# Four column tiles for the small products of a recurrent attention, and wide-attention steps moved to the front

## The chip, the cores and the metric

The kernel runs on one core of a Trainium2 chip. A core has a matrix engine (TensorE, "PE" in the profile; its weight loads are "PEld"), VectorE ("DVE"), ScalarE ("ACT"), GpSimd ("POOL"), a queue engine (SyncE, "SP") and 16 DMA engines. The metric is device time in microseconds; lower is better.

TensorE's array has 128 rows and 128 columns. It can be used whole ("full" below, 128*128 in the profile) or in tiles that work side by side: 128*64 is half the columns ("half"), 128*32 a quarter of them ("col"), 64*128 half the rows ("tall"), 32*128 a quarter of the rows ("row"). Four products that fill the four quarters are called a quartet here.

## The reference

Two attentions over the same 2048 tokens are mixed by a gate per token. The first is recurrent: 64 segments of 32 tokens, each with 8 memory tokens in front, and the first 8 output rows of a segment are the memory of the next. The second is a plain softmax attention with 32 heads of 18.

```python
def _A_ref(x, mem0, Wq, Wk, Wv, Wo, seg_len):      # 32 heads of 128, Dm 576
    ...
    for s in range(n_seg):                          # 64 segments
        xs = x[:, s * seg_len:(s + 1) * seg_len, :].copy()
        h = jnp.concatenate([mem, xs], axis=1)      # 8 + 32 tokens
        q = jnp.einsum('btd,dhe->bhte', h, Wq)
        k = jnp.einsum('btd,dhe->bhte', h, Wk)
        v = jnp.einsum('btd,dhe->bhte', h, Wv)
        scores = jnp.einsum('bhqe,bhke->bhqk', q, k) * scale
        scores = jnp.where(mask[None, None], scores, -1000000000.0)
        p = _softmax(scores, axis=-1)
        o = jnp.einsum('bhqk,bhke->bhqe', p, v)
        o = jnp.einsum('bhte,hed->btd', o, Wo)
        mem = o[:, :M, :].copy()
        outs.append(o[:, M:, :])
    return jnp.concatenate(outs, axis=1)

g = _sigmoid((x * gate_w).sum(-1, keepdims=True))
a = _A_ref(x, A_mem0, A_Wq, A_Wk, A_Wv, A_Wo, A_seg_len)
b = _B_ref(x, B_wqkv, B_wo)                         # softmax attention, 32 heads of 18
return g * a + (1 - g) * b
```

## The kernel before, in words

**The order is planned.** Nothing is issued as it is written. Every operation is handed to `add` with its engine, an assumed duration, what it depends on, a priority and, for TensorE, the tile mode. `Plan.run` then places the operations one by one on five engines by these assumed durations, and the instructions are emitted in that order, so each engine's queue is fixed when the program is built. Among the operations that can start, the lowest priority number goes first; for TensorE a change of tile mode adds `RANK["switch"]`. Most priorities come from the table `RANK`. Where the plan sees TensorE wait for long enough while a wide-attention accumulation is open, it puts in a filler: a product of zeros that adds nothing to the bank `ob` (`warm_col`, L773, and `warm_full`, L779; "obW" and "filler" below).

**First stage.** All tokens are transposed (ptx). TensorE computes the wide attention's queries and keys (pq, `project_qk`, 36 units of five products) and values (pvb, `project_v`, 32 units). The evacuations of these units, in the order in which they are written, are the list `beats`. The results go through DRAM (qtd, ktd, vgd) and come back as tiles of one group of four heads (qch, kch, vch). `load_weights` brings the recurrent weights in 12 slices (Wv, then Wq, then Wk, four each) on GpSimd's DMA queue; slice number k waits for evacuation 2 + 4k, by a marker that VectorE writes (L530). The gate's products are pgs. When the first stage's memory is free, `open_rest` opens the second stage's tiles with memsets on GpSimd.

**The wide attention** is 512 visits: 8 groups of four heads, 4 chunks of 512 queries (group and chunk together are `gq`, 0 to 31), 16 blocks of 128 keys. A visit is four row-tiled products of scores into sb (L801), one exponential over 128x2048 on ScalarE into etb (L810), and four column-tiled products with the values into ob (L819). There is one sb buffer of four banks, so the next scores wait for the exponential. After 16 visits VectorE normalises the chunk and GpSimd stores it (otd).

**The recurrence** is 64 steps. In each, 8 memory tokens and the first 24 new tokens (32 in all) are projected: Q, K and V in two halves, each of five quartets with 512 columns (pvv, L1126). Q and K are transposed by DMA (tt<-tm, issued on SP) and copied into qk. The last 8 tokens of a segment need no memory, so their projections are done apart: the *last units* (`last_unit`, pv, L896 and L900), one for each of 4 groups of 16 segments (q), of Q, K and V, and of 8 column blocks. A value unit is five products with 512 columns, a Q or K unit 20 products with 128. They go through DRAM (vld, qkd) and return as xl and v_sb. Then, for each half of the heads: scores psh (L1215, 16 products of 64 columns of weights by 40), exponential, masking by a minimum, sums over each pair of heads pss (L1241, three full products by 2), reciprocal, spreading prb (L1258, six half products by 128), multiplication, values pso (L1279, tall), copies to ot, and the output projection acc (L1040, quartets by 144). The fold (pw, L1327 to L1329, three full products) turns the first 8 output rows back into the next step's input ht. Every fourth step the last tokens' outputs are projected too.

**Pacing.** `seg_gate[s]` is the first pvv of step s. The first `RANK["ahead"]` visits are free of it (62 before); the others are spread evenly over the 64 steps, each tied to its step's gate. Last units of group q + 1 are handed in during the 16 steps of group q, 24 over 15 of the 16.

**The end.** The recurrent output is read back from DRAM, GpSimd multiplies its 16 blocks of 128 tokens by the gate (L1469), TensorE does the wide output projection (po, L1482 and L1486), VectorE adds both, and SP stores.

Of the kernel before, what the change touches and what calls it, by code (L numbers as in the profile page):

```python
# [16 lines left out]
RANK = {  # L17
    "switch": 0.563, "near": 0, "early": 0.35, "wait": 0.363, "Q0": 1.228, "K0": 2.187, "Q1": 3.003,
    "K1": 2.432, "V0": 4.793, "V1": 5.753, "t0": 4.121, "t1": 0.488, "ph0": 6.882, "ph1": 0.05, "sm0": 1.292,
    "sm1": 0.349, "bc0": 1.798, "bc1": 1.166, "po0": 0.486, "po1": 0.474, "op0": 6.496, "op1": 0.107,  # L20
    "fo": 0.097, "lo0": 9.11, "lo1": 2.155, "la": 2.226, "ob": 0.587, "eQ": 8.858, "eK": 1.861, "eV": 1.477,
    "co": 0.886, "le": 6.512, "xp": 7.097, "mn": 0.05, "ct": 3.886, "fin": 16.522, "la_gate": 1, "lo_gate": 1,
    "ahead": 62, "behind": 0, "tail": 0.404, "qc": 2.731, "gap": 0, "cool": 7.325,
}


class Op:
# [3 lines left out]
        "engs", "dur", "fn", "deps", "prio", "mode", "take", "give", "tail",  # L31
        "eng", "start", "end", "left", "users", "name", "seq", "slots", "dmas", "kb",
    )
# [11 lines left out]
class Plan:  # L45
# [42 lines left out]
    def add(  # L88
        self, name, engs, dur, fn, deps=(), prio=5.0, mode=None, take=(), give=(), tail=0.0, dmas=0, kb=0.0
    ):  # L90
        op = Op(name, engs, dur, fn, deps, prio, mode, take, give, tail)
        op.dmas, op.kb = dmas, kb
        op.seq = len(self.ops)
        op.slots = {}
        self.ops.append(op)
        return op
# [7 lines left out]
    def run(self):  # L104
        free = self.free = {e: 0.0 for e in ("PE", "DVE", "ACT", "POOL", "SP")}
        waiting = {e: [] for e in free}
        mode = None
# [8 lines left out]
        order = []  # L116
        n = len(self.ops)
# [5 lines left out]
        while len(order) < n + extra:  # L123
# [11 lines left out]
            if pick == "PE" and open_ and self.warm is not None:  # L135
                for m in ("col", "full"):
                    if m not in (mode, op.mode):
                        continue
                    turn = 0.0 if mode == m else self.SWITCH
                    done = sum(d for t, d in recent if t > free["PE"] - 2.5)  # L140
                    if est - free["PE"] < self.WARM + turn + RANK["gap"] or done > RANK["cool"]:
                        continue
                    w = Op("warm", "PE", self.WARM, self.warm[m], [], 9.0, m, (), (), 0.0)
                    w.dmas, w.kb, w.slots, w.left = 0, 0.0, {}, 0
                    w.eng, w.start, w.end = "PE", free["PE"], free["PE"] + self.WARM + turn
                    free["PE"], mode = w.end, m
                    recent.append((w.end, self.WARM))
                    order.append(w)
                    extra += 1
                    pick = None  # L150
                    break
                if pick is None:
                    dirty = {"PE"}
                    continue
# [7 lines left out]
            if pick == "PE":  # L162
                if op.mode != mode:
                    dur += self.SWITCH
                mode = op.mode
                if op in self.opens:
                    open_ = True
                if op in self.closes:
                    open_ = False
                recent = recent[-8:]  # L170
                recent.append((est, dur * self.ARRAY[mode]))
            op.end = est + dur
# [86 lines left out]
def kernel(  # L259
# [15 lines left out]
    nc = tc.nc  # L275
# [252 lines left out]
    def behind(name, beat, corner, n, fn, deps, tail):  # L528

        mark = add(f"mk{name}", "DVE", 0.07, lambda e: nc.vector.memset(corner(), 0.0), [beat, *deps], prio=0.05)  # L530
        before = paced[-1:]
        op = add(name, "POOL", 0.7 * n, fn, [mark, *deps, *before], prio=0.15, tail=5.5)
        paced.append(op)
        return op

    def load_weights():
        k = 0
        for w, src, name in ((wv, A_Wv, "wv"), (wq, A_Wq, "wq"), (wk, A_Wk, "wk")):
            w2 = src.rearrange("d h e -> d (h e)")
            weight_loads[name] = []  # L540
            for c in range(NF):
                def load_w(e, w=w, w2=w2, c=c):
# [10 lines left out]
                weight_loads[name].append(  # L553
                    behind(f"{name}{c}", beats[2 + 4 * k], lambda w=w, c=c: w[0][0:1, 0, c, 0:1], 3, load_w, [], 5.5)
                )
# [230 lines left out]
    for gq in range(GB * NQC):  # L786
        g, qc = divmod(gq, NQC)
        load_q(gq)
        for kb in range(NKB):
# [15 lines left out]

            vi = add(f"sb{gq}.{kb}", "PE", 0.216, visit, [k_of[c], q_of[gq], last_vi], prio=0.0, mode="row", take=("sb",))

# [6 lines left out]
            def values(e, c=c, gq=gq, kb=kb, o=o):  # L814
# [11 lines left out]
            va = add(  # L826
                f"ob{gq}.{kb}", "PE", 0.216, values, [ex, v_of[c], last_va], prio=RANK["ob"], mode="col",
                take=("ob",) if kb == 0 else (), give=(("etb", ex, 0),),
# [54 lines left out]
    last_ops = []  # L883

    def last_unit(q, kind, b, prio, gate_dep):
        cols = slice(q * P, (q + 1) * P)
        j, hf = divmod(b, 2)

        def part(k):
            def fn(e):  # L890
# [3 lines left out]
                if kind == 2:  # L894
                    rw, cc = w_slice(wv, k, b * 512, 512)
                    nc.tensor.matmul(pv[:, :], lhsT=xL[:, cc, cols], rhs=rw, start=(k == 0), stop=(k == NF))  # L896
                    return
                for c in range(NF + 1):
                    lw, cc = w_slice((wq, wk)[kind], c, (4 * b + k) * Dh, Dh)
                    nc.tensor.matmul(  # L900
                        pv[:, k * P:(k + 1) * P], lhsT=lw, rhs=xL[:, cc, cols], start=(c == 0), stop=(c == NF)
                    )
            return fn
# [5 lines left out]
        for k in range(NF + 1 if kind == 2 else NF):  # L909
            a = add(  # L910
                f"la{tag}.{k}", "PE", 0.216 if kind == 2 else 5 * 0.057, part(k), [a] if a else deps,
                prio=prio - (0.01 if a else 0.0), mode="full", take=() if a else ("pb",),
            )
            parts.append(a)
# [56 lines left out]

    opening = add("open", "POOL", 5.0, open_rest, b_work + early, prio=0.5)

# [81 lines left out]
    group_end = {}  # L1055
    pend_lo = []

    for s in range(n_seg):
# [124 lines left out]
        for hf in range(2):  # L1183
# [25 lines left out]
            def psh(e, hf=hf, s=s):  # L1209
                box["psh", s, hf] = ph = bank([P, W8], FP32, "psh")  # L1210
                qk = opened["qk"]
                for r in range(8):
                    for jj in range(2):
                        k = jj * 8 + r
                        nc.tensor.matmul(  # L1215
                            ph[64 * jj:64 * jj + 64, r * L:(r + 1) * L],
                            lhsT=qk[:, hf, 1, k * L:k * L + 64], rhs=qk[:, hf, 0, k * L:(k + 1) * L],
                            start=True, stop=True, tile_position=(0, 64 * jj),
                        )

            p_ = add(f"ph{hf}.{s}", "PE", 0.41, psh, [*turned, pl], prio=RANK[f"ph{hf}"], mode="half", take=("pb",))
            cur[f"psh{hf}"] = p_

# [14 lines left out]
            def sm(e, hf=hf, s=s):  # L1238
                box["pss", s, hf] = ps = bank([P, 6], FP32, "pss")
                for k, o in enumerate(CH):  # L1240
                    nc.tensor.matmul(  # L1241
                        ps[:, 2 * k:2 * k + 2], lhsT=opened["et", hf][:, o:o + P], rhs=bsel[:, :], start=True, stop=True
                    )

            s_ = add(f"sm{hf}.{s}", "PE", 0.1, sm, [m_], prio=RANK[f"sm{hf}"], mode="full", take=("pb",))

# [7 lines left out]
            def bc(e, hf=hf, s=s):  # L1254
                box["prb", s, hf] = pr = bank([P, W8], FP32, "prb")
                for k, o in enumerate(CH):
                    for jj in range(2):
                        nc.tensor.matmul(  # L1258
                            pr[64 * jj:64 * jj + 64, o:o + P],
                            lhsT=box["rq", s, hf][:, 2 * k + jj:2 * k + jj + 1].to_broadcast([P, 64]),  # L1260
                            rhs=ident[:, :], start=True, stop=True, tile_position=(0, 64 * jj),
                        )

            b_ = add(f"bc{hf}.{s}", "PE", 0.2, bc, [r_], prio=RANK[f"bc{hf}"], mode="half", take=("pb",))

# [57 lines left out]
        if s + 1 < n_seg:  # L1323
            def fold(e, s=s):
                box["pw", s] = pw_ = bank([P, NF + 2, M], FP32, "pw")
                obf, bd = box["obf", s], opened["bd"][:, :, :].rearrange("p a r -> p (a r)")
                nc.tensor.matmul(pw_[:, 0:NF, :], lhsT=obf[:, 0:P], rhs=selm, start=True, stop=True)  # L1327
                nc.tensor.matmul(pw_[:, NF, :], lhsT=bd[:, TL:3 * TL], rhs=sel[:, :], start=True, stop=True)
                nc.tensor.matmul(pw_[:, NF + 1, :], lhsT=bd[:, 0:2 * TL], rhs=sel[:, :], start=True, stop=True)  # L1329

            fo = add(f"fo{s}", "PE", 0.1, fold, [c1, c2], prio=RANK["fo"], mode="full", take=("pb",))
            cur["fold"] = fo
# [51 lines left out]
        if i4 == 3:  # L1384
            lo_deps = [hist[s - k]["otl"] for k in range(4)]
            pend_lo.append((s, gi, lo_deps))
            if s == n_seg - 1:
                last_out(*pend_lo.pop(), None)
        if s < 48:
            q = s // 16 + 1  # L1390
            lo, hi = (s % 16) * 24 // 15, min(24, (s % 16 + 1) * 24 // 15)
            if s % 16 == 15:
                lo = hi = 24
            order = [(2, b) for b in range(8)] + [(k, b) for b in range(8) for k in (0, 1)]
            for kind, b in order[lo:hi]:
                last_unit(q, kind, b, RANK["la"], gates_of[RANK["la_gate"]])


# [160 lines left out]
```

## Time and profile before

| what | us |
|---|---|
| median of three runs (1497.04 to 1503.77) | 1502.29 |
| the profiled execution's own time | 1500.88 |
| its span | 1499.2 |
| first visit's scores start | 45.0 |
| first step's first projection (pvv) starts | 136.05 |
| last product (pw) of the fold of step 0, 46, 62 | 180.4, 1130.8, 1443.4 |
| ScalarE, 512 exponentials over 128x2048, 1.877 each | 961.2 busy |
| TensorE, fillers L773 and L779 | 60.6 and 24.6 busy |
| last weight slice issued | 129.3 |

The profile is one execution. Its page gives the busy time of each engine, then the span in 40 slices of 37.5 us with a digit for the busy tenths, the granted clock of TensorE ("PEclk", tenths of full speed) and the share of DMA. A timeline lists instructions in order of time: start, length, engine, line, operation, output<-inputs, tile of the array as rows*columns, shape, count, and in brackets the idle time before it with what ended it. Matmuls of one queue overlap, so lengths do not add up; distances between starts do.

### The profile page before, as it was taken

What the parts mean: (1) busy time and instruction counts of PE and PEld (TensorE: products, weight loads), DVE (VectorE), ACT (ScalarE), POOL (GpSimd) and SP (SyncE); (2) the same over time, 40 slices, a digit from 0 to 9 for tenths busy, and PEclk for the clock granted to TensorE, in tenths of its full rate; (3) what the DMA queues carried; (4) which work ended last, traced back from release to release, by engine and by line L of the source; (5) the groups of instructions that cost most, each with busy time, mean ns of one, the idle gap of its engine ahead of it and who ended that gap; (6) DMA issues with size and microseconds to landing.
All of it is one profiled execution on the core that took longest, in us unless ns stands there. A gap on an engine that the chain in (4) does not pass through costs nothing.

```text
span 1499.2 us, 68540 instructions
## 1 busy us (share of the span) xinstructions
PE 1388.5 (93%) x30405; PEld 763.4 (51%) x30435; DVE 833.4 (56%) x2033; ACT 1053.4 (70%) x760; POOL 553.2 (37%) x1166
## 2 busy tenths in 40 slices
PE   7689899999999999999999999999999999998997
PEld 4345444555555445555555544555554545454445
DVE  6244455665655555665555555565655555554555
ACT  2125687777777787777777877777777777776770
POOL 7222124423352324433352325333453225333235
PEclk9799999999999999999999999999999999999999
DMA  8865633433233333333333333323333324333344
GB/s 269 260 233 171 163 64 77 74 58 67 59 75 68 59 61 70 75 66 61 69 69 60 70 54 79 69 57 68 71 73 80 53 57 68 59 56 47 47 112 125
DMA packets 343380, 130.09 MB, mean 87 GB/s; under 512 B 296943, under 2 KB 329159, under 8 KB 343083
## 3 DMA queue, kind: packets, MB, share of 16 engines
q1 hardware_dynamic: 314843, 81.22, 28.1%
q0 software_dynamic: 27088, 43.31, 10.7%
q8 instruction: 238, 3.90, 1.1%
q10 hardware_dynamic: 1152, 1.18, 0.3%
q14 instruction: 59, 0.48, 0.1%
HBM read 52.74 MB, written 30.86 MB: 56 GB/s over the span
## 4 chain that ended last, share of the span: by engine, by line
PE 66%; ACT 13%; DMA 10%; DVE 6%; issue 3%; POOL 1%; SPq 0%; ACTq 0%; DVEq 0%
PE pvv L1126 24%; ACT etb L810 13%; PE sb L801 11%; PE acc L1040 8%; PE ob L819 7%; DMA tt<-tm 6%; PE pv L900 4%; PE pq L608 2%; PE psh L1215 2%; DVE tm L418 2%; PE pv L896 2%; PE ob L773 1%; PE pso L1279 1%; DMA vgd<-vt 1%; PE prb L1258 1%
## 5 line engine op out<-in xcount | busy, mean ns | idle before, releaser
L810 ACT ACTIVATE etb<-sb 128x2048 bf16<-128x2048 f32 x512 | 961.2, 1877 | 332.6 <-PE sb L801 311.7
L418 DVE CAST tm<-pvv 128x512 bf16<-128x512 f32 x360 | 248.3, 691 | 256.8 <-PE pvv L1126 250.0
L1126 PEld LDWEIGHTS <-ht 128*32 128x32 bf16 x7680 | 206.8, 97 | 185.2 <-DVE ht L1335 10.6
L801 PE MATMUL sb<-qch,kch 32*128 32x512 bf16 x2048 | 205.8, 386 | 33.7 <-ACT etb L810 20.3
L819 PE MATMUL ob<-etb,vch 128*32 128x512 bf16 x2048 | 205.3, 390 | 1.9 <-issue 1.4
L1077 POOL COPY ht<-xg 128x96 bf16<-128x96 bf16 x64 | 17.3, 270 | 418.2 <-PE pvv L1126 398.9
L1040 PE MATMUL acc<-wo,ot 128*32 128x144 bf16 x8192 | 160.4, 228 | 3.2 <-issue 2.3
L1040 PEld LDWEIGHTS <-ot 128*32 128x32 bf16 x8192 | 135.3, 97 | 23.0 <-issue 9.2
L801 PEld LDWEIGHTS <-kch 32*128 32x128 bf16 x2048 | 65.5, 91 | 149.0 <-issue 121.8
L1126 PE MATMUL pvv<-wq_m,ht 128*32 128x512 bf16 x2048 | 140.2, 380 | 0.8 <-DVE ht L1335 0.8
L1126 PE MATMUL pvv<-wv_m,ht 128*32 128x512 bf16 x2048 | 139.6, 379 | 0.7 <-DVE tm L418 0.7
L1126 PE MATMUL pvv<-wk_m,ht 128*32 128x512 bf16 x2048 | 136.5, 379 | 0.9 <-DVE vl L418 0.9
L418 DVE CAST ot<-pso 128x320 bf16<-128x320 f32 x216 | 98.6, 482 | 54.7 <-PE pso L1279 54.3
L819 PEld LDWEIGHTS <-vch 128*32 128x32 bf16 x2048 | 53.0, 93 | 103.2 <-issue 101.7
L1199 DVE COPY qk<-tt 128x512 bf16<-128x512 bf16 x256 | 76.7, 306 | 43.1 <-DMA tt<-tm 40.7
L1095 POOL COPY qk<-xl 128x256 bf16<-128x256 bf16 x128 | 50.4, 401 | 92.8 <-PE psh L1215 79.4
L1268 DVE TENSOR_TENSOR et<-et,prb 128x320 bf16<-128x320 bf16 x128 | 61.2, 480 | 36.0 <-PE prb L1258 33.5
L722 POOL DMA_DIRECT2D qch<-qtd x120 | 60.8, 514 | 49.1 <-PE sb L801 45.4
L722 POOL DMA_DIRECT2D otd<-stage x124 | 62.6, 512 | 31.6 <-DVE stage L862 26.4
L1166 DVE COPY v_sb<-tm 32x512 bf16<-32x512 bf16 x234 | 70.5, 301 | 6.1 <-ACT tm L416 0.3
L722 POOL DMA_DIRECT2D kch<-ktd x112 | 56.7, 513 | 43.4 <-PE sb L801 43.2
L1215 PEld LDWEIGHTS <-qk 128*64 128x64 bf16 x2048 | 45.0, 112 | 51.4 <-issue 38.8
(149 smaller groups left out, 1860.7 us busy)
## 6 DMA issues: line engine op xcount, KB each, us to landing
xl<-qkd SPq DMA_DIRECT2D x64, 128.0 KB
v_sb<-tm SPq DMA_DIRECT2D x256, 32.0 KB
qkd<-vl POOLq DMA_DIRECT2D x48, 128.0 KB, 2.7
wo<-in_A_Wo_dram POOLq DMA_DIRECT2D x4, 1152.0 KB, 8.8
vgd<-vt SPq DMA_DIRECT2D x32, 128.0 KB
wv_m<-in_A_Wv_dram POOLq DMA_DIRECT2D x4, 1024.0 KB, 8.2
wq_m<-in_A_Wq_dram POOLq DMA_DIRECT2D x4, 1024.0 KB, 7.5
wk_m<-in_A_Wk_dram POOLq DMA_DIRECT2D x4, 1024.0 KB, 7.5
```

What stands on the lines that cost most here:

```text
L418: nc.vector.tensor_copy(out=out_of(), in_=in_of())
L722: dma(out=rows_, in_=pads) if out else dma(out=pads, in_=rows_)
L801: nc.tensor.matmul(sb[:, j, :], lhsT=kc[r, o:o + P], rhs=qt_[r, :], start=True, stop=True, tile_position=(32 * j, 0),)
L810: nc.scalar.activation(out=etb[:, :, :], in_=box["sb", gq, kb][:, :, :], func=ACT.Exp, scale=scale_b)
L819: nc.tensor.matmul(ob[32 * j:32 * j + 32, :], lhsT=vc[:, o + 32 * j:o + 32 * j + 32], rhs=etb[:, j, :], start=(kb == 0), stop=(kb == NKB - ...
L900: nc.tensor.matmul(pv[:, k * P:(k + 1) * P], lhsT=lw, rhs=xL[:, cc, cols], start=(c == 0), stop=(c == NF))
L1040: nc.tensor.matmul(acc[32 * j:32 * j + 32, :], lhsT=o[:, slot, t0:t0 + CT], rhs=wo[:, h, RW * j:RW * j + RW], start=(first and s_ == 0), s ...
L1126: nc.tensor.matmul(pv[32 * j:32 * j + 32, :], lhsT=ht[:, cc, :], rhs=rw, start=(c == 0), stop=(c == NF), tile_position=(0, 32 * j), skip_g ...
L1166: move(out=opened["v_sb"][64 * (j // 2):64 * (j // 2) + CT, o:o + 512], in_=tm[32 * j:32 * j + CT, :],)
L1199: eng.tensor_copy(out=opened["qk"][:, hf, a, 0:16 * L].rearrange("p (j i t) -> p j i t", i=4, t=L)[:, :, :, 0:CT], in_=box["tt", s, a, hf] ...
L1215: nc.tensor.matmul(ph[64 * jj:64 * jj + 64, r * L:(r + 1) * L], lhsT=qk[:, hf, 1, k * L:k * L + 64], rhs=qk[:, hf, 0, k * L:(k + 1) * L], ...
L1268: nc.vector.tensor_tensor(out=et[:, :], in0=et[:, :], in1=box["prb", s, hf][:, :], op=ALU.mult)
```

## The change

Five things change.

1. The products of psh, pss, prb and the fold, and those of the last units of groups 1 to 3, are issued as quartets of column tiles; only pso (tall), sb (row) and the first and last stages' products keep another mode. Group 0 of the last units stays full.
2. Visits of `gq` 0 and 1 (the first 32) get priorities -0.6 and -0.5, below everything else; `ahead` is 32.
3. The weight slices wait for evacuations 12, 16, 18, 23, 26, 30, 34, 38, 43, 48, 53 and 57, and the opening of the second stage waits for their issue.
4. Last units of groups 1 to 3 stand in one list, and two are handed in at step 0 and at every step that is not a multiple of four.
5. All of `RANK` is new, and some assumed durations of the plan. Fillers are no longer limited by `cool`; the assumed load of an operation on the array can be given by `use`.

```diff
 RANK = {
...
-    "ahead": 62, "behind": 0, "tail": 0.404, "qc": 2.731, "gap": 0, "cool": 7.325,
+    "ahead": 32, "behind": 0, "tail": 0.162, "qc": 6.688, "gap": 0.024, "cool": 766.744,
 }
...
-                    behind(f"{name}{c}", beats[2 + 4 * k], lambda w=w, c=c: w[0][0:1, 0, c, 0:1], 3, load_w, [], 5.5)
+                    behind(f"{name}{c}", beats[(12, 16, 18, 23, 26, 30, 34, 38, 43, 48, 53, 57)[k]], lambda w=w, c=c: w[0][0:1, 0, c, 0:1], 3, load_w, [], 3.0)
...
-            vi = add(f"sb{gq}.{kb}", "PE", 0.216, visit, [k_of[c], q_of[gq], last_vi], prio=0.0, mode="row", take=("sb",))
+            vi = add(f"sb{gq}.{kb}", "PE", 0.216, visit, [k_of[c], q_of[gq], last_vi], prio=-0.6 if gq < 2 else 0.0, mode="row", take=("sb",))
...
-                f"ob{gq}.{kb}", "PE", 0.216, values, [ex, v_of[c], last_va], prio=RANK["ob"], mode="col",
+                f"ob{gq}.{kb}", "PE", 0.216, values, [ex, v_of[c], last_va], prio=-0.5 if gq < 2 else RANK["ob"], mode="col",
...
+    def tiled(q, out_, lw, rw, c):
+        if q == 0:
+            nc.tensor.matmul(out_, lhsT=lw, rhs=rw, start=(c == 0), stop=(c == NF))
+            return
+        for i in range(4):
+            r = slice(32 * i, 32 * i + 32)
+            nc.tensor.matmul(
+                out_[r, :], lhsT=lw[:, r], rhs=rw, start=(c == 0), stop=(c == NF),
+                tile_position=(0, 32 * i), skip_group_check=True,
+            )
...
-    opening = add("open", "POOL", 5.0, open_rest, b_work + early, prio=0.5)
+    opening = add("open", "POOL", 4.0, open_rest, b_work + early + paced, prio=0.5)
...
                 for r in range(8):
-                    for jj in range(2):
-                        k = jj * 8 + r
+                    for i in range(4):
+                        k, o = (i // 2) * 8 + r, 32 * (i % 2)
                         nc.tensor.matmul(
-                            ph[64 * jj:64 * jj + 64, r * L:(r + 1) * L],
-                            lhsT=qk[:, hf, 1, k * L:k * L + 64], rhs=qk[:, hf, 0, k * L:(k + 1) * L],
-                            start=True, stop=True, tile_position=(0, 64 * jj),
+                            ph[32 * i:32 * i + 32, r * L:(r + 1) * L],
+                            lhsT=qk[:, hf, 1, k * L + o:k * L + o + 32], rhs=qk[:, hf, 0, k * L:(k + 1) * L],
+                            start=True, stop=True, tile_position=(0, 32 * i), skip_group_check=True,
                         )
...
                 for k, o in enumerate(CH):
-                    nc.tensor.matmul(
-                        ps[:, 2 * k:2 * k + 2], lhsT=opened["et", hf][:, o:o + P], rhs=bsel[:, :], start=True, stop=True
-                    )
+                    for i in range(4):
+                        nc.tensor.matmul(
+                            ps[32 * i:32 * i + 32, 2 * k:2 * k + 2],
+                            lhsT=opened["et", hf][:, o + 32 * i:o + 32 * i + 32], rhs=bsel[:, :],
+                            start=True, stop=True, tile_position=(0, 32 * i), skip_group_check=True,
+                        )
...
-            for kind, b in order[lo:hi]:
+        if s == 0 or s % 4:
+            for q, kind, b in units[:2]:
                 last_unit(q, kind, b, RANK["la"], gates_of[RANK["la_gate"]])
+            del units[:2]
```

prb and the fold are cut into quartets in the same way. With the built program's order, TensorE has 30,435 products before and 38,670 after, fillers included (283 and 335 filler groups).

## The prediction

> **What bounds the kernel now.** I read the page's first two parts, then TensorE's own timeline inside one step, then the stretches of the opening, then GpSimd at the end.
>
> ```profile
> PE 1388.5 (93%) x30405; PEld 763.4 (51%) x30435; DVE 833.4 (56%) x2033; ACT 1053.4 (70%) x760; POOL 553.2 (37%) x1166
> PE   7689899999999999999999999999999999998997
> ACT  2125687777777787777777877777777777776770
> PEclk9799999999999999999999999999999999999999
> DMA  8865633433233333333333333323333324333344
> ```
>
> TensorE is busy from the fifth slice on, ScalarE is nearly idle in the first three slices, and DMA is at 0.8 there. The three regions have three limits.
>
> ```profile
> 604.04 0.39 PE L1126 MATMUL pvv<-wv_t,ht 128*32 128x512 bf16 x4
> 604.36 0.43 PE L1215 MATMUL psh<-qk 128*64 128x40 bf16 x16
> 604.73 0.39 PE L801 MATMUL sb<-qch,kch 32*128 32x512 bf16 x4
> 605.05 0.40 PE L819 MATMUL ob<-etb,vch 128*32 128x512 bf16 x4
> ...
> 606.23 0.22 PE L1241 MATMUL pss<-bsel,et 128*128 128x2 bf16 x3
> 606.31 0.38 PE L900 MATMUL pv<-xL,wq_m 128*128 128x128 bf16 x4
> ...
> 607.33 0.36 PE L1258 MATMUL prb<-ident,rq 128*64 128x128 bf16 x6
> 607.63 0.39 PE L801 MATMUL sb<-qch,kch 32*128 32x512 bf16 x4
> ...
> 610.69 0.42 PE L1040 MATMUL acc<-wo,ot 128*32 128x144 bf16 x16
> 611.05 0.37 PE L1279 MATMUL pso<-et,v_sb 64*128 64x40 bf16 x16
> 611.35 0.93 PE L1040 MATMUL acc<-wo,ot 128*32 128x144 bf16 x48
> ```
>
> Columns: start in us, length, engine and line, operands, tile of the array (rows*columns), shape, count. What a group costs is the distance from its start to the next start, not its length. Four column tiles with 512 columns take 0.22 (603.83 to 604.04 in the same view). From sb (row tiles) to ob (column tiles) is 0.32, so a change of tile mode costs 0.10; over all such pairs I use 0.097. Without that change: psh 0.27 for eight pairs of 64 columns, 34 ns a pair; pss 0.08 for three full products, 27 ns each; prb 0.20 for three pairs, 62 to 67 ns; acc 0.25 for four quartets, 62 ns a quartet; pso 0.20 for eight pairs, 26 ns.
>
> ```profile
> 25.00:50.00 25.00, 15.18 (x86) 7.92 (x84) 7.31 (x18) 2.37 (x3) 9.48 (x24) 0.82 0.84 268
> 75.00:100.00 25.00, 19.20 (x118) 10.61 (x116) 10.07 (x23) 4.15 (x3) 3.56 (x6) 0.86 0.77 258
> 45.04 2.24 PE L801 MATMUL sb<-qch,kch 32*128 32x512 bf16 x4 [7.58 <-DMA kch<-ktd]
> ```
>
> The first two lines are stretches: length, busy time of PE, PEld, DVE, ACT and POOL, granted clock, DMA share, GB/s. In the opening the limit is transfers; TensorE idles, waits 7.58 us for the first key tile, and its granted clock is 0.82 to 0.86.
>
> **The sum by stretch.** I cut the run at the last small product (pw) of three steps. Time is from the trace; "issue" adds each built group at the prices above, fillers and mode changes included.
>
> | stretch | time before | issue before | issue after |
> |---|---|---|---|
> | to the fold of step 0 | 180.4 | 125.5 | 135.8 |
> | steps 1 to 46 | 950.4 | 874.1 | 862.2 |
> | steps 47 to 62 | 312.6 | 277.8 | 280.6 |
> | rest | 55.8 | 41.2 | 45.9 |
>
> They add to the 1499.2 us span; its own run took 1500.88, 1.4 below the median of 1502.29, so 1.7 lie outside the span.
>
> **Column tiles.** The built order has 1,762 mode changes before and 1,271 after. In steps 1 to 46 they fall from 1249 to 850: 399 x 0.097 = -38.7. What is paid: each of these 46 steps now issues 25 small quartets (16 psh, 6 pss, 3 pw) in place of 16 pairs and 9 full products. The trace has no quartet under 144 columns. Its cost lies between 34 ns (no worse than psh's pair, the four loads overlapping) and 62 ns (acc). By product, pso's pair gives 13.4 ns; I take four of them, 54 ns. Then 1150 x 0.054 = 62.1 stands for 46 x 0.79 = 36.2 (psh 0.54, pss 0.15, fold 0.09), +25.9. The last tokens' 960 products with 128 columns cost 56 ns full (605.38 to 605.67 for five); as quartets 56 to 62, I take the upper end, +5.3. prb: no change. Together -7.5 in this stretch; with all small quartets at 34 ns -37, at 62.5 about +4. The 512-wide value units keep 0.22. In steps 47 to 62 the same terms give -12.0 and +9.0.
>
> The Trainium skill speaks against this edit: TensorEngine Tiling (Array Packing), Instruction Overhead, says that a product costs about 60 cycles however few columns it has and that one should not split a dimension that is already small. An estimate from that page, four times 25 ns in series, would make a quartet 100 ns. The acc row, four in 62 ns, disagrees for four column tiles; no run here shows it at 2 to 40 columns.
>
> **First 32 visits moved.** A visit is sb, the exponential and ob. The built order has 30 before the first pvv (13 before) and 40 by the fold of step 0 (27 before). This takes 22 visits' excess, 0.43 each, out of steps 1 to 46 (366 to 344): -9.4; it gives +1.6 to 47 to 62. In the opening 13 x 0.43 + 31 x 0.097 and about 2 more add 10.3. Cover: 180.4 - 125.5 = 54.9 us in which TensorE idled or ran below full clock, and ScalarE was busy 2.4 of 25 us. Without that cover it costs +10.3. Between the gate's products (pgs) and the last tokens' first unit a visit follows every ten pq or fifteen pvb products, 2.9 us, while sb to sb with the exponential (1.88) takes 2.4 to 2.5; the ScalarE chain fits. On GpSimd the first weight slice (issued at 27.6, the fourth by 40.4) now waits for the evacuation of the fifth value block, behind which the first q and k tiles load; so I expect some of the 7.58 us back. All 12 slices now stand ahead of the memsets that open the second stage; before, the last was issued at 129.3, after them. The first store of the wide attention's output stands ahead of the last slice, too. SP's order is nearly unchanged. I take -4 for the opening, bounds -12 and +10.
>
> **Spread last tokens, new ranks.** Two units in every step but each fourth, in place of 24 over 15 of 16 steps: the same products, no price of its own. Fillers (zero products) rise by 5.6 in steps 1 to 46 and 3.9 in 47 to 62. They stand where the plan sees TensorE wait; I count half. 48 evacuations move from VectorE to ScalarE (about 26 us over the run) and 32 copies of v_sb to GpSimd; both idle enough (L810 follows 332.6 us of idle), and cost nothing unless a visit is late: 0.6 each then.
>
> **The end.** GpSimd multiplies 16 blocks of the recurrent part by the gate (L1469), 1.71 each.
>
> ```profile
> 1473.58 0.39 POOL L1379 COPY otl<-ot 128x256 bf16<-128x256 bf16 x1
> 1473.96 1.71 POOL L1469 TENSOR_SCALAR wq_m<-wk_m,gsb 128x576 f32<-128x576 bf16 x1
> ```
>
> Eleven of them stand ahead of this copy, fifteen after the change: +6.8. But a copy of v_sb (1.39, from 1453.32) that the first one waited behind is gone, and the acc products behind the copy, which took 8 us between others, stand together (2.0). Twelve visits, not seven, follow the last fold: 12 x 2.45 = 29, still inside the copy's place, which was 30 us after the fold and is 37 then. I take 0, bounds -5 and +7.
>
> **Sum.** Steps 1 to 46: -11.9, less half the fillers, -15. Steps 47 to 62: +2.8 - 1.9, +1. Opening -4, end 0: -18, span 1481, run **1483**.
>
> **Rivals.**
> 1. *The opening becomes TensorE's (slower).* Place: from pgs to the first pvv. In issue time the first pvv moves from 90.5 to 98.8. If the visits' loads come late, pq products wait behind them in order, evacuations come later, and with them the weight slices that wait for those. Price: the 10.3 in full and two more landings of 6.3 (a qtd store's, in the chain of waits) ahead of the last key slice, 12.6: +23, with 14 taken off behind it: 1510. It decides when the first pvv starts after 150 us. For: DMA at 0.84 and slices up to the 58th evacuation. Against: the same bytes, ScalarE idle.
> 2. *The saved changes turn into waits.* A step is a chain (projections, transposes by DMA, softmax, output, fold) with about 1.7 us of idle in 20.7. Steps 47 to 62 had 7 visits and still 19.5 us, 2.2 idle. Then steps keep their time, only the opening gains: 1497.
> 3. *Small quartets overlap fully* (34 ns): -30 more in steps 1 to 46 and -8.6 in 47 to 62, two thirds of it reaching the end: 1457. For: within a quartet products start 4 ns apart.
> 4. *They do not overlap*: four full-mode products of 26 ns, 102 ns a quartet: 1597 x 0.048 = +77, 1560. Against: acc.
>
> **How the numbers follow.** Forecast 0.42 (own range 1470 to 1494), rivals 0.2, 0.18, 0.16, 0.04. Half a per cent is about what a measurement of this kernel can tell. Faster: the forecast nearly whole, rival 3 and a fifth of rival 2, 0.61; same: most of rival 2 and part of rival 1, 0.18; slower 0.21. The range reaches to rivals 1 and 3: 1454 to 1512.
>
> **What would show it.** Right: mode changes worth 0.1 us gone around psh, prb, pv; eight psh quartets in 0.43; first pvv between 125 and 140 with 30 visits done; fold of step 46 near 1111; end 55 us after the last fold. Wrong: step times as before with larger waits of sb or pss (rival 2); first pvv after 150 (rival 1); psh quartets near 34 or 100 ns (rivals 3, 4).

## The result and the profile after

The changed kernel takes 1549.59 us (median of four runs, 1542.61 to 1556.49) where the kernel before takes 1499.66 beside it (1495.91 to 1503.77). The ratio is 1.033, with a 95% interval of 1.027 to 1.040: slower, where I had forecast 1483. The profiled execution took 1542.61, its span 1540.9.

The same cuts as in the prediction, at the last pw product of three folds, show where the 41.7 us between the two profiled executions went (the medians lie 50 us apart; of the changed kernel's four executions the fastest was profiled):

| stretch | before | after | difference | forecast |
|---|---|---|---|---|
| to the fold of step 0 | 180.4 | 186.5 | +6.1 | -4 |
| steps 1 to 46 | 950.4 | 976.1 | +25.7 | -15 |
| steps 47 to 62 | 312.6 | 315.4 | +2.8 | +1 |
| rest | 55.8 | 62.9 | +7.1 | 0 |

The page of the changed kernel, first two parts:

```profile
PE 1383.4 (90%) x38670; PEld 757.2 (49%) x38670; DVE 802.3 (52%) x1954; ACT 1074.4 (70%) x807; POOL 578.9 (38%) x1198
PE   7798899899889999989889999888899998899996
ACT  2455477777777777777677777777777777777771
PEclk9899899999999999999999999999999999999998
DMA  6896433333333234333333333332334333433262
```

TensorE is busy for 5 us less than before, although it issues 8,235 products more (30 of those before are missing in the records). The span is 42 us longer. From the fifth slice on its row has thirteen eights where there were two, the granted clock is not lower, and no other engine is near full. So TensorE waits more, and the question is for what. The parts on the queues and on the chain of waits answer it; first the kernel before:

```profile
q8 instruction: 238, 3.90, 1.1%
PE 66%; ACT 13%; DMA 10%; DVE 6%; issue 3%; POOL 1%; SPq 0%; ACTq 0%; DVEq 0%
L1040 PE MATMUL acc<-wo,ot 128*32 128x144 bf16 x8192 | 160.4, 228 | 3.2 <-issue 2.3
```

and the changed kernel:

```profile
q8 instruction: 302, 4.95, 1.3%
PE 61%; DMA 12%; issue 9%; DVE 8%; ACT 7%; POOL 2%; SPq 0%; POOLq 0%; ACTq 0%; DVEq 0%
L1051 PE MATMUL acc<-wo,ot 128*32 128x144 bf16 x8192 | 161.1, 227 | 24.7 <-issue 23.7
```

"issue" is time in which an engine waits for nothing that the profile shows. It rises from 3% to 9% of the chain (16.7 us of that are one piece in the end stage, told below), and the output projection, whose products wait for nothing once they have begun, has 23.7 us of such idle time (2.3 before). The first line is the queue that brings TensorE's own instructions, with packets, MB and share. TensorE issues two instructions per product, a weight load and the product: with about 100 waits for other engines, 60,975 of them in the records before and 77,433 after. Divided by 256 these are 238.2 and 302.5, so a packet holds 256 instructions, and 4.95 MB / 302 is 16 KiB a packet. The change made a quarter more code, and the code has to come in blocks of 256.

One step of the changed kernel, TensorE's timeline:

```profile
367.55 0.24 PE L1257 MATMUL pss<-bsel,et 128*32 128x2 bf16 x12
367.63 0.40 PE L893 MATMUL pv<-xL,wk_m 128*32 128x128 bf16 x16
...
368.18 0.35 PE L1276 MATMUL prb<-ident,rq 128*32 128x128 bf16 x12
368.47 0.40 PE L803 MATMUL sb<-qch,kch 32*128 32x512 bf16 x4
368.79 0.24 PE L1051 MATMUL acc<-wo,ot 128*32 128x144 bf16 x3
370.52 0.66 PE L1051 MATMUL acc<-wo,ot 128*32 128x144 bf16 x29 [1.48 <-issue]
371.11 0.37 PE L1297 MATMUL pso<-et,v_sb 64*128 64x40 bf16 x16
```

The array work is as cheap as one could wish: the 12 products of pss take 0.08 us, three quartets of 27 ns. But after 3 of the 32 products of an output projection TensorE stands still for 1.48 us, in the middle of a quartet. No data is missing there: neither the product behind the gap nor its weight load carries a wait. In the whole trace 94 of some 107 gaps over 0.3 us inside a run of one line stand at the instruction whose number is 194 or 195 modulo 256: a border of blocks, not a place in the algorithm.

**How a block comes.** In the records of the queue, a packet takes 1.05 us, and products resume 1.2 to 1.6 us after its end. Successive packets start at least 3.29 us apart (first percentile; 3.35 before), and the next is started only when TensorE has crossed the border before it, to within some 30 instructions: one block lies ahead, no more. What counts is therefore how long 256 instructions last in each kind of work: pvv 128 products x 54 ns = 6.9 us, acc 128 x 15.5 ns = 2.0 us, small quartets 128 x 7 ns = 0.9 us. Below some 3.4 us TensorE runs dry. By the mean there is no shortage (302 blocks x 3.4 us = 1027 us of 1541); it is the dense phases that starve, one behind the other around the softmax and the output projection, and the long projections cannot store up for them.

The Trainium skill (Runtime: NRT & Kernel Launch, Instruction fetch mechanics) gives the same 16 KiB and 256 instructions, and says that crossing a border is "mostly hidden", because issue is slower than the fetch. The first agrees with this trace (256 instructions and 16 KiB a packet), the second does not: the standstills add up to 76.3 us in steps 1 to 46, as the next table shows.

I summed what the trace shows of it: the distance between two successive products beyond what their shapes cost, where it is over 0.1 us, put down to the fetch if the later one starts 1.1 to 1.75 us after a packet's end, and to other waits if not.

| us of waiting (places) | before | after |
|---|---|---|
| steps 1 to 46, by the fetch | 17.1 (48) | 76.3 (103) |
| steps 47 to 62, by the fetch | 3.3 (9) | 15.4 (20) |
| steps 1 to 46, other | 45.9 | 45.7 |

The fetch explains +59.2 where the stretch grew by 25.7; the difference, 33.5, is what the cheaper array work and 22 visits fewer in the stretch gave back. The other waits are the same in these two kernels, but the two differ in their order as well as in their tiles; experiments 1 and 2 take these apart.

**The opening.** Two lines of the changed kernel:

```profile
135.33 1.04 PE L1141 MATMUL pvv<-wq_m,ht 128*32 128x512 bf16 x16
151.56 0.38 PE L889 MATMUL pv<-xL,wk_m 128*128 128x128 bf16 x4 [4.46 <-ACT vl L418]
```

The first pvv comes at 135.33 (136.05 before) with 30 visits done instead of 13, and the first scores at 38.4 instead of 45.0. But the profiled execution of the kernel before is late here. Numbers 1, 4 and 9 below have its opening and reach the first pvv at 131.4 to 132.6 and the fold of step 0 at 177.3 to 178.5; numbers 2, 3, 5, 6, 7 and 10 have the changed opening and reach them at 135.7 to 141.2 and 184.7 to 191.0. So the changed opening costs about 9 us, not 6 (on one chip: 177.5 and 178.5 against 185.8 and 187.0), and about half of that lies ahead of the first pvv. Behind it, group 0's K units wait for buffers of vl, which are still being stored to DRAM: 4.46 us here and 4.07 at 164. The first scores of the recurrence (psh) start at 176.0 (169.3 before; 164.7 to 166.6 in numbers 1, 4 and 9).

**The end.** Timeline of the changed kernel, GpSimd and TensorE:

```profile
1513.24 0.39 POOL L1405 COPY otl<-ot 128x256 bf16<-128x256 bf16 x1
1530.38 1.72 POOL L1491 TENSOR_SCALAR wq_m<-wk_m,gsb 128x576 f32<-128x576 bf16 x1 [16.75 <-DMA wk_m<-a_dram]
```

```profile
1511.60 9.36 PE L1504 MATMUL po<-xL,wq_m 128*128 128x288 bf16 x75
1520.89 0.61 PE L821 MATMUL ob<-etb,vch 128*32 128x512 bf16 x8
1521.33 2.17 PE L1051 MATMUL acc<-wo,otl 128*32 128x144 bf16 x128
```

The copy is 35.3 us behind the last fold (30.2 before). Its 128 acc products do not start when it is done: they stand behind 75 products of the wide output projection in TensorE's order, 7.7 us more. The store, the reading back (16.75 us of waiting on GpSimd) and the last gate product follow from there. Numbers 2, 3, 5, 6, 7 and 10, with the same order, take 60.5 to 62.4 us behind the last fold, number 1, with the tiles in the order before, 55.9: the order costs this, not the tiles.

### The profile page after: what moved, and what is told of

Its sections match the earlier page's. It is cut to its first block, busy times and chain, and to the rows that moved or that the text cites. A ratio compares the mean times of both kernels' runs of the same rounds, so it can differ in the third digit from the quotient of the medians.

```text
span 1540.9 us, 85064 instructions
## 1 busy us (share of the span) xinstructions
PE 1383.4 (90%) x38670; PEld 757.2 (49%) x38670; DVE 802.3 (52%) x1954; ACT 1074.4 (70%) x807; POOL 578.9 (38%) x1198
## 3 DMA queue, kind: packets, MB, share of 16 engines
q8 instruction: 302, 4.95, 1.3%
## 4 chain that ended last, share of the span: by engine, by line
PE 61%; DMA 12%; issue 9%; DVE 8%; ACT 7%; POOL 2%; SPq 0%; POOLq 0%; ACTq 0%; DVEq 0%
PE pvv L1141 20%; PE acc L1051 10%; PE sb L803 9%; DMA tt<-tm 8%; ACT etb L812 7%; PE ob L821 6%; PE pv L893 3%; PE ob L775 3%; DVE tm L420 2%; PE pso L1297 2%; PE pq L610 2%; PE psh L1230 1%; PE prb L1276 1%; PE pv L889 1%; DVE qk L1214 1%
## 5 line engine op out<-in xcount | busy, mean ns | idle before, releaser
L420 DVE CAST tm<-pvv 128x512 bf16<-128x512 f32 x339 | 233.7, 690 | 245.9 <-PE pvv L1141 241.4
L1141 PEld LDWEIGHTS <-ht 128*32 128x32 bf16 x7680 | 200.8, 97 | 199.6 <-issue 20.4
L1051 PE MATMUL acc<-wo,ot 128*32 128x144 bf16 x8192 | 161.1, 227 | 24.7 <-issue 23.7
L803 PEld LDWEIGHTS <-kch 32*128 32x128 bf16 x2048 | 61.5, 91 | 166.4 <-issue 144.7
L420 DVE CAST ot<-pso 128x320 bf16<-128x320 f32 x205 | 93.0, 480 | 51.9 <-PE pso L1297 51.2
L775 PE MATMUL ob<-unit,nil 128*32 128x512 bf16 x1336 | 110.1, 381 | 1.8 <-issue 1.7
L1214 DVE COPY qk<-tt 128x512 bf16<-128x512 bf16 x256 | 83.5, 331 | 52.7 <-DMA tt<-tm 50.7
L1286 DVE TENSOR_TENSOR et<-et,prb 128x320 bf16<-128x320 bf16 x128 | 61.7, 486 | 45.0 <-PE prb L1276 41.7
L1329 DVE CAST obf<-acc 128x144 bf16<-128x144 f32 x64 | 19.7, 308 | 115.7 <-PE acc L1051 115.7
```

The costliest lines, as they stand in the source:

```text
L420: nc.vector.tensor_copy(out=out_of(), in_=in_of())
L775: nc.tensor.matmul(box["ob"][32 * j:32 * j + 32, :], lhsT=nil[:, 0:32], rhs=unit[:, :].unsqueeze(1).to_broadcast([P, 4, P]), start=False, ...
L803: nc.tensor.matmul(sb[:, j, :], lhsT=kc[r, o:o + P], rhs=qt_[r, :], start=True, stop=True, tile_position=(32 * j, 0),)
L1051: nc.tensor.matmul(acc[32 * j:32 * j + 32, :], lhsT=o[:, slot, t0:t0 + CT], rhs=wo[:, h, RW * j:RW * j + RW], start=(first and s_ == 0), s ...
L1141: nc.tensor.matmul(pv[32 * j:32 * j + 32, :], lhsT=ht[:, cc, :], rhs=rw, start=(c == 0), stop=(c == NF), tile_position=(0, 32 * j), skip_g ...
L1214: eng.tensor_copy(out=opened["qk"][:, hf, a, 0:16 * L].rearrange("p (j i t) -> p j i t", i=4, t=L)[:, :, :, 0:CT], in_=box["tt", s, a, hf] ...
```

## The experiments

Theories: **F**, TensorE starves for instructions; **O**, the new order (visits in front, spread units, ranks) is what costs; **A**, small quartets are dear on the array. Each ratio is to the kernel before on the same chip, with its 95% interval.

**1 and 2: order and tiles apart.** The first gives the kernel before the new quartets and leaves its order; the second keeps the changed order and issues the old full and half products in it.

```diff
 # r1, in the kernel before (pss, prb, fold, last units alike)
-                    for jj in range(2):
+                    for i in range(4):
...
-                            start=True, stop=True, tile_position=(0, 64 * jj),
+                            start=True, stop=True, tile_position=(0, 32 * i), skip_group_check=True,
 # r2, in the changed kernel: the same lines the other way
```

> The kernel before, its order and ranks untouched, with the new quartets in psh, pss, prb, the fold and the last units of groups 1 to 3 (15,550 more TensorE instructions, 61 more blocks of 256). Theory (TensorE starves for instructions: one fetch of 256 at a time, never under 3.3 us apart): slower than before, 1515 to 1540; about 480 mode changes saved (-47) and psh a little cheaper (-6), against some 70 of stalls at block borders. Rival (the new order and the moved visits cost the time, quartets pay): faster than before, 1455 to 1485.

Measured: 1535.95, ratio 1.027 (1.025 to 1.029), 299 blocks, as the theory of the fetch has it.

> The changed kernel, its order, ranks and visits untouched, with the old full and half products back. Theory (instruction fetch): faster than the changed kernel, 1510 to 1535, stalls at block borders back to about 20 us, mode changes back. Rival (the new order): as slow as the changed kernel or slower by the mode changes, 1550 to 1590.

Measured: 1486.22, ratio 0.994 (0.992 to 0.995), 242 blocks: faster than either theory had it, since neither counted a gain of the order itself. From the pages of these two, the tiles alone first:

```profile
q8 instruction: 299, 4.90, 1.3%
PE 61%; ACT 13%; DMA 10%; DVE 8%; issue 6%; POOL 1%; SPq 0%; ACTq 0%; DVEq 0%; POOLq 0%
```

```profile
q8 instruction: 242, 3.96, 1.1%
PE 71%; DMA 10%; ACT 8%; DVE 4%; issue 4%; POOL 2%; SPq 0%; POOLq 0%; ACTq 0%; DVEq 0%
```

The tiles cost 2.7% by themselves, and the order gains 0.6%: O falls as the cause. A falls with the timeline above, where a quartet of pss takes 27 ns. The order without tiles has 1,919 mode changes, 157 more than before, and is still faster. The profiled executions by stretches, in us:

| stretch | before | 1: tiles | 2: order | both |
|---|---|---|---|---|
| to the fold of step 0 | 180.4 | 177.5 | 185.8 | 186.5 |
| steps 1 to 46 | 950.4 | 985.8 | 931.2 | 976.1 |
| steps 47 to 62 | 312.6 | 310.7 | 306.2 | 315.4 |
| rest | 55.8 | 55.9 | 60.5 | 62.9 |
| steps 1 to 46, fetch waits | 17.1 | 68.1 | 12.5 | 76.3 |
| steps 1 to 46, other waits | 45.9 | 53 | 31 | 45.7 |

The order loses in the opening and at the end. It gains in the steps, and in steps 1 to 46 nearly all of its 19 us are other waits that are gone. There the tiles cost 35 us in the order before and 45 in the changed one. In both the fetch waits grow by more than that (51 and 64), the other waits grow too (8 and 14), and the cheaper array work gives back some 24 and 33.

**3: fewer instructions, same useful work.** The filler of four column tiles becomes one of one tile: 2,004 instructions fewer in TensorE's queue. This also lightens the array, so it doesn't isolate the fetch by itself.

```diff
 def warm_col
-        for j in range(4):
+        for j in range(1):
```

> The changed kernel with each filler cut from four column tiles to one: the same 0.22 us each, the same order, 2,004 fewer instructions (8 blocks). Theory (instruction fetch): 8 to 20 us faster, 1530 to 1542. Rival (order, or the cost of quartets): no change, 1550.

Measured: 1522.79, ratio 1.020 (1.017 to 1.022), against 1.033 for the changed kernel; 294 blocks. That is more than expected. Fetch waits fall by 10.7 us in steps 1 to 46 and by 1.5 in 47 to 62, some 12 of the 20.5 by which the span fell; where the rest comes from stays open.

**4: the fetch by itself.** Behind the last product of the kernel before, 512 quartets with two columns, into a bank that nothing reads.

```diff
+    for n_ in range(512):
+        for j in range(4):
+            nc.tensor.matmul(
+                extra[32 * j:32 * j + 32, 0, 0:2], lhsT=nil[:, 0:32], rhs=unit[:, 0:2], start=True, stop=True,
+                tile_position=(0, 32 * j), skip_group_check=True,
+            )
```

> The kernel before with 512 quartets of 2 columns (4,096 instructions, 16 blocks) after its last product, into a bank that nothing reads. Theory (instruction fetch): the burst takes about 3.35 us a block, some 49 us on TensorE, and the span grows by about 41. If only the array or the issue of single instructions sets the pace (27 ns a quartet, as pss in the changed kernel): 14 us on TensorE, span + 6.

TensorE's timeline in this kernel:

```profile
1488.60 1.67 PE L1525 MATMUL sb<-unit,nil 128*32 128x2 bf16 x188
1492.26 1.19 PE L1525 MATMUL sb<-unit,nil 128*32 128x2 bf16 x128 [1.99 <-issue]
1495.73 1.18 PE L1525 MATMUL sb<-unit,nil 128*32 128x2 bf16 x128 [2.28 <-issue]
1499.20 1.19 PE L1525 MATMUL sb<-unit,nil 128*32 128x2 bf16 x128 [2.29 <-issue]
1502.95 1.19 PE L1525 MATMUL sb<-unit,nil 128*32 128x2 bf16 x128 [2.56 <-issue]
...
1542.01 0.68 PE L1525 MATMUL sb<-unit,nil 128*32 128x2 bf16 x68 [2.29 <-issue]
```

This is the whole mechanism in six lines. 188 products run at once: 60 that were left of the block under way and one block of 128 ahead. From then on 128 products, 256 instructions, run in 1.19 us and the next 2 to 2.6 us are empty: a block every 3.47 us in ten of the fourteen cases and every 3.75 in four, at best 13.6 ns for an instruction. In a case of 3.47 the next packet starts 1.1 us after TensorE has gone into a block, takes 0.9, and the products resume 1.5 after its end; why these steps take so long, no run shows. The 4,096 instructions take 54 us. Inside a block the array takes 32 ns a quartet here, and at that price they would have taken 16. The span became 1543.7 us, 44.5 more than before (one execution of each), near the 41 of the theory and far from the 6 of its rival.

**5 and 6: parts of the tiles undone** in the changed kernel. In the first the last units are full products again; in the second, besides, psh is in halves and the filler has one tile, so that of the quartets only pss, prb and the fold are left.

```diff
-                    tiled(q, pv[:, :], xL[:, cc, cols], rw, k)
+                    nc.tensor.matmul(pv[:, :], lhsT=xL[:, cc, cols], rhs=rw, start=(k == 0), stop=(k == NF))
```

> The changed kernel, order untouched, with the last units alone back in full products: 6,480 fewer instructions (25 blocks), 299 more mode changes. Theory (instruction fetch): stalls fall by some 45, mode changes give back 20 to 29, so 1525 to 1540, faster than the changed kernel. Rival (only the pieces of the softmax, which lie on the chain of a step, hurt): mode changes alone, 1560 to 1580.

Measured: 1513.61, ratio 1.008 (1.006 to 1.011), a larger gain than expected. The units alone bring 2.5% back: 6,480 instructions fewer, and fetch waits of 34.6 in steps 1 to 46 in place of 76.3.

> The changed kernel, order untouched, last units full, psh in halves, fillers of one tile; only pss, prb and the fold stay quartets: 64,903 instructions, 1,729 mode changes. Theory (instruction fetch): stalls near those before (25 to 30), 1480 to 1500. Rival (mode changes rule): slower than the run with old tiles by nothing and by less than it has fewer changes, 190 x 0.097 = 18 faster than 1486, 1468.

Measured: 1512.17, ratio 1.006 (1.004 to 1.009): a miss, no better than the one before it. Against number 7, which differs by these three kinds of quartet, it has 19 blocks more and is 1.8% slower. Steps 1 to 46 are 22.5 us longer; 14.8 of that are fetch waits, 9.2 other waits. These quartets stand in the chain of the softmax, where each standstill makes the next engine late; that this is why a few blocks cost so much is argued, not shown.

**7 to 9: the order and the fillers.** Number 7 is number 2 with one-tile fillers. Number 8 is number 2 planned anew with the old priorities of the first 32 visits. Number 9 is the kernel before with one-tile fillers, 1,188 instructions fewer.

```diff
 # r8
-... visit, [k_of[c], q_of[gq], last_vi], prio=-0.6 if gq < 2 else 0.0, mode="row", take=("sb",))
+... visit, [k_of[c], q_of[gq], last_vi], prio=0.0, mode="row", take=("sb",))
```

> The changed order with all old products and fillers of one tile: 59,929 instructions (8 blocks fewer than the run with old tiles at 1486). Theory (instruction fetch): 3 to 12 us faster, 1474 to 1483, less than the 27 that the same edit gave with quartets, since only about 18 us of stalls are left. Rival (the narrower fillers help in another way, the same with any products): 27 faster, 1459.

Measured: 1485.55, ratio 0.988 (0.984 to 0.992), the fastest of all; 234 blocks, fetch waits of 10.5 in steps 1 to 46. By the ratios it gains some 8 us on number 2, as the theory has it, and not 27.

> The changed kernel with old products and without the priorities that put the first 32 visits in front (planned anew, ahead still 32). If the moved visits give the gain of the new order (9.4 us of visits out of steps 1 to 46): slower than 1486 by 5 to 12, 1491 to 1498. If they cost (opening and end): 1475 to 1483.

Measured: 1512.15, ratio 1.006 (1.004 to 1.008). By stretches, number 8 against number 2: 176.8 and 185.8, 940.5 and 931.2, 308.1 and 306.2, 79.1 and 60.5. It is slower than either expectation, and it does not isolate the moved visits, since the whole plan is new: number 8 has 22 of the 512 visits done by the fold of step 0 (40 in number 2), 350 in steps 1 to 46 (344) and 26 behind the last fold (12). With 18 visits more, number 2's opening is 9.0 us longer. The 1.2% is the end: 18.6 us, with 14 visits more left over in number 8. The 9.3 us in steps 1 to 46 come with 6 visits only.

> The kernel before with fillers of one tile: 1,188 fewer instructions (4.6 blocks), order untouched. Theory (instruction fetch): 0 to 8 us faster than before, since its stalls at block borders sum to about 21. Rival (narrow fillers help by something else than the instruction count): 16 faster, the 27 of the changed kernel by the share of its fillers (198 of 334).

Measured: 1497.79, ratio 1.000 (0.998 to 1.002): nothing. Where the fetch waits are small, fewer instructions bring nothing.

**10 to 12: what the fillers and the plan are worth**, all from the changed kernel with the old products: the same order and no fillers at all; one-tile fillers and `ahead` at 40, planned anew; one-tile fillers and the plan made with the modes and durations that the old products have.

```diff
 # r10: warm_col and warm_full issue nothing
 # r11
-    "ahead": 32, "behind": 0, "tail": 0.162, "qc": 6.688, "gap": 0.024, "cool": 766.744,
+    "ahead": 40, "behind": 0, "tail": 0.162, "qc": 6.688, "gap": 0.024, "cool": 766.744,
 # r12 (prb, pss, fold and units alike)
-            p_ = add(f"ph{hf}.{s}", "PE", 0.44, psh, ..., mode="col", take=("pb",), use=0.3)
+            p_ = add(f"ph{hf}.{s}", "PE", 0.41, psh, ..., mode="half", take=("pb",))
```

> The changed order with old products and no fillers at all: 670 fewer instructions than with fillers of one tile, and TensorE idle where they stood. If the fillers only fill waits: within 5 us of the run with one-tile fillers (0.988 of before). If they stand in the way of work: up to 20 us faster. If TensorE's granted clock falls without them: slower, and the clock under 0.95.

Measured: 1500.97, ratio 1.004 (1.001 to 1.006). The mean granted clock is 0.962, where number 2 has 0.989 and the changed kernel 0.987; the fall is smaller than expected. It is not spread evenly. Steps 47 to 62 of this run, then of number 7, as a stretch with TensorE's busy time, granted clock, DMA share and GB/s:

```profile
1114.00:1437.00 323.00, 291.85 (x6768) 0.91 0.32 55
```

```profile
1111.00:1417.00 306.00, 296.13 (x6889) 1.00 0.34 58
```

This stretch is 17 us longer at a clock of 0.91, while steps 1 to 46 take 927.1 us at 0.99 to 1.00 where number 7 takes 926.1. So the fillers do hold the clock, and their worth lies in the last steps, where the last units have run out.

> The changed order, old products, one-tile fillers, ahead 40 in place of 32 (planned anew): eight more visits free of a step's gate, share 7.375 a step. If the end (62 us after the last fold, 56 before) is long for the visits left over: it falls by 3 to 6, ratio 0.985. If another chain sets the end: as with 32, 0.988.

Measured: 1488.13, ratio 0.994 (0.992 to 0.996): no better than 32. The end does fall by 4.7 us, from number 7's 61.8 to 57.1, but the stretches ahead of it are 17 us longer (by the profiled executions, which lie 12.5 us apart where the ratios give 8).

> As the run with old products and one-tile fillers, but planned with the old modes and durations too, so the plan knows of the mode changes. If the order that was planned for column tiles costs by its needless mode changes (1,919 against 1,823): 5 to 10 us faster, ratio 0.982 to 0.985. If not: 0.988 to 1.0.

Measured: 1516.33, ratio 1.012 (1.008 to 1.016): a miss. Told the truth about the products, the planner finds a worse order: steps 1 to 46 take 953.0 us where number 7 takes 926.1, and as much, some 27 us, is added to the waits that are not the fetch (about 50 against 23). Why this plan waits more stays open.

## Why the prediction was wrong, point by point

- **The step that failed** is the sum itself: "issue adds each built group at the prices above". The prices are those of the array. 256 instructions have a price too, 3.4 to 3.5 us, which the sum puts at nothing, and a stretch with a lower array price per block pays that instead. The fetch waits added 59.2 us in steps 1 to 46 and 12.1 in 47 to 62. The kernel before already had 20 of them, so its trace could have told: q8's 238 packets, 3.35 us apart at the least, and "issue" behind acc.
- **Mode changes**: built as counted, 1,271. No run has them alone. In steps 1 to 46, three pairs of one order leave, after fetch and other waits are taken off, 24 us for 334 changes fewer (before and number 1), 33 for 460 (number 2 and the changed kernel) and 31 for 290 (number 5 and the changed kernel): 0.07 to 0.11 each, with the prices below in it, so the 0.097 is about right.
- **Small quartets**, taken at 54 ns: too high. pss takes 27 ns a quartet, psh about 30, prb about 60, near the 62 to 67 of its pairs; that is the price of rival 3, which would have made the kernel 1457. The right price for the array made the result worse, since a quartet of 27 ns uses up 8 instructions that take 109 ns to come (8 x 13.6). The estimate of 100 ns from the Trainium skill (TensorEngine Tiling (Array Packing), Instruction Overhead) does not hold on the array, where pss has 27 and the burst of number 4 has 32; its advice not to split a small dimension holds here for another reason, the instructions. From its own terms the prediction's two bounds for this stretch come out as about -36 and +2, not -37 and +4; nothing hung on that.
- **Units**, +5.3: undoing them alone took steps 1 to 46 from 976.1 to 951.2, so in place they cost about 25, fetch and all.
- **Visits moved**: -9.4 forecast for steps 1 to 46. No run measures it: numbers 8 and 2 differ by 9.3 us there, but by 6 visits and not by 22, so that the two figures agree is luck. "Without that cover it costs +10.3" is near the 9.0 of numbers 2 and 8, and near the 9 us by which the changed opening is longer over all runs: the 54.9 us in which TensorE idled or ran below full clock did not hide it. Opening: -4 forecast, +6.1 measured, inside its bounds. Rival 1's sign, a first pvv after 150, did not come (135.33, and at most 141.2 in the other runs), nor did its price. A part of what it names, more work ahead of the first pvv, is open: about half of the loss lies there.
- **The end**, 0 forecast with +7 as upper end: +7.1. The copy is later by 5.0, where 6.8 was forecast. But the acc products behind it, taken as a gain of 6 (2.0 in place of 8), end 9.9 us behind the copy (8.1 before): the forecast had not looked at what stands ahead of them in TensorE's queue.
- **Rival 2**, saved time turning into waits: the waits that are not the fetch do grow with the tiles, by 8 us in the order before and by 14 in the changed one, but the steps did not keep their time, they grew.
- **What would show it**: first pvv and its 30 visits right; eight psh quartets about 0.24, not 0.43; the fold of step 46 at 1162.6, not 1111; the end 62.9 behind the last fold, not 55.

## What to carry to other kernels

Count instructions as well as array time: of this kernel's TensorE stream, every 256 (weight loads and products together) need about 3.4 us, with one block ahead, so a phase whose instructions cost less than 13.6 ns on the array, and which is longer than the block that lies ahead, runs at the pace of the fetch. Cutting a product into four column tiles gives four times the instructions. With 512 columns a block of them lasts 6.9 us and the fetch keeps up; where the products are short and stand together, the cut costs. A stretch of one execution can be some us off, as the opening before was here: look at the other runs that share it before naming a cause. When a change has several parts, cross the largest two first: order and tiles apart showed at once that the one gains and the other loses, and the changed order with the old products and one-tile fillers (number 7) is 1.2% faster than the kernel before (0.988, 0.984 to 0.992).

## What the runs showed of the hardware

- TensorE's instructions come in 16 KiB packets of 256 (238 before, 302 after), at best one every 3.3 to 3.5 us, one ahead.
- Four column-tile products of two columns, loads included, take 27 ns (pss) to 32 ns (number 4) together while instructions last.
- Without zero products in the waits the mean granted clock fell from 0.989 to 0.962, and in steps 47 to 62 from 1.00 to 0.91.
